# One fused attention kernel: some of VectorE's integer adds on GpSimd, planner constants, and a re-ordered end

## The chip, the core and the metric

The kernel runs on one core of one Trainium2 chip. The metric is the device time of one execution in microseconds; lower is better. A core has five engines that run their own instruction streams and meet at semaphores: TensorE (PE in the profile; its weight loads are PEld), VectorE (DVE), ScalarE (ACT), GpSimd (POOL) and SyncE (SP), which here issues most of the transfers.

## What is computed

Two attention blocks read the same x (2,048 rows of 512). Block A is softmax attention with 32 heads of width 16, block B is linear attention with the same heads, and a gate per row mixes them. Cut to what matters:

```python
qkv = (x @ wqkv).reshape(B, S, 3, H, Dh).transpose(2, 0, 3, 1, 4)
# A
scores = einsum("bhqd,bhkd->bhqk", q, k) * Dh ** -0.5
a = (einsum("bhqk,bhkd->bhqd", softmax(scores), v)) @ wo_A
# B
phi = lambda t: where(t > 0, t + 1, exp(t)) + 1e-6
kv = einsum("bhsd,bhse->bhde", phi(k), v); z = phi(k) summed over s
b = (einsum("bhqd,bhde->bhqe", phi(q), kv) / (phi(q) . z + 1e-6)) @ wo_B
g = sigmoid((x * gate_w).sum(-1))
out = g * a + (1 - g) * b
```

## The kernel before

**Units and rounds.** The scores of block A are cut into 2,048 units. A unit is one product of 128 keys by 512 queries of one head, and fills one PSUM bank (128 x 512, float32). 64 units make a round (one query chunk, four heads), and there are 32 rounds. The main loop goes over groups of units: two slots of three banks (`SLOTS`) take turns; TensorE fills the banks of a slot, ScalarE raises all units of the slot to the exponential in one instruction (L1979, 1,024 or 1,536 columns) and writes them to the tile PT, and TensorE multiplies them with the values (`pv_cols`, into one accumulator bank) while ScalarE works on the other slot.

**Claimed units.** VectorE takes a part of the units from ScalarE. `claim` gives a unit to VectorE; the operation at L1518 scales a PSUM bank and writes it as 16-bit integers into a buffer of the tile DP, and these bits are read as 16-bit floats, a piecewise-linear approximation of the exponential. Four claimed units share one buffer (a group, `tri`, 2,048 columns). To make the approximation better, `try_close` writes two more copies of the whole buffer with a constant added to the integers (`STEPS` 342 and 683, the operation at L1566), in two further buffers, and TensorE sums the three with scaled values. So a claimed unit needs three value products where a unit of ScalarE needs one. There are 13 buffers (`NB`); `free_buffers` lists those that nothing reads or writes any more. `claim_round` takes a unit of the current round while at least 14 (`MIN_LEFT`) of its units are left, and of the next round after that.

**The planner.** The order of all instructions is fixed when the kernel is built. The builder keeps an estimated clock for each engine (`E.t`), with an estimated duration for each operation. VectorE's work waits in a list (`items`) with a priority: 0 for the accumulator, 1 for PSUM evictions and claims, 2 for the range check, 3 for the adds; `pump` emits the next one when VectorE's estimated clock falls behind TensorE's. An item can also be marked for GpSimd (a sixth field, its duration); before, these are only the 12 products of normalisation at L1246 (`POOL_TT` = 1.3), which `pool_go` emits behind an add. `est_start` puts a VectorE operation that reads no PSUM bank behind the estimated end of a running GpSimd operation (`pool_runs`); this orders the plan and adds no semaphore. `claim_beside`, `claim_in_group` and `misc_step` decide whether a unit is claimed, by the work that VectorE has queued (`dve_load` against `CLAIM_LOAD`, `RING_LOAD`, `STARVE`). Projections, block B and output products are steps in chains with a due time in groups (`target`, `late`). `misc_step` runs them in TensorE's spare time, and `fill` adds products of a zero tile (`warm`) when TensorE's estimated share of work falls under `MAC_LOW` (`MAC_END` from 44 units of a round on).

The branch for adds on GpSimd exists in `try_close` before the change, but `EVERY = 0` turns it off.

**The end.** After the last round VectorE normalises the last heads into O_sb (L1275), TensorE transposes it, and VectorE adds it into OT (L2050). TensorE finishes the last four output blocks of 128 rows. For two of them (0 and 1) everything but the last product has been summed in `presum`, and VectorE finishes them (L2075). The other two (2 and 3) are finished by ScalarE (L2069). For block 2 seven products are left for the end (`late_fns`). A check (L2055, L2080, L2085) tests whether all row sums were in range; its flag decides a branch on every engine to a general version of the kernel.

Of the kernel before, what the change touches and what calls it, by code (L numbers as in the profile page):

```python
# [53 lines left out]
NTRI = 4  # L54
# [150 lines left out]
def d_sb(n, rate=1.0):  # L205
    return 0.15 + n * 1.042e-3 * rate
# [6 lines left out]
def bass_gated_mix__mha_block__linear_attn_block__prompt_kernel(  # L213
# [29 lines left out]
    PRE_T = 5  # L243
    PRE_GAP = 8
    OUT_GAP = 8

    with ExitStack() as es:
# [62 lines left out]
        dev = SB([128, 2, 128], FP32, "dev")  # L310
        flag = SB([128, 1], I32, "flag")
        epool = SB([128, 2, 512], BF16, "epool")
        KVbd = SB([128, NCC, 128], BF16, "KVbd")
# [81 lines left out]
        r_rraw = [R(f"rraw{k}") for k in range(8)]  # L395
        r_dev, r_flag = R("dev"), R("flag")
        r_e = [R("e0"), R("e1")]
        r_phiK = [[R(f"phiK{s}_{k}") for k in range(4)] for s in range(2)]
# [33 lines left out]
        pool_runs = collections.deque(maxlen=4)  # L432
        POOL_SOON = 0.3
        POOL_TT = 1.3
        POOL_V = 0.9
        POOL_ADD = 2.4
        EVERY = 0
        OT_POOL = 1
# [37 lines left out]

        def pool_go(sync):

            for it in sorted(items, key=lambda i: i.seq):
                o = it.ops[0]  # L480
                if len(o) > 5 and not blocked(it, o[1], o[2]) and est_start(PO, o[1], o[2]) <= DV.t + POOL_SOON:
                    STATS["pool"] = STATS.get("pool", 0) + 1
                    emit_item_op(it, sync)
                    return
# [48 lines left out]

        WAIT_BANK = 0.12

        def pump(now, look=0.25):
            try_close()
            while items and DV.t <= now + look:
                best = None
                for it in items:  # L540
                    o = it.ops[0]
                    if len(o) > 5 or blocked(it, o[1], o[2]):
                        continue
                    st = est_start(DV, o[1], o[2])
                    wait = st - DV.t
                    key = (wait > (WAIT_BANK if it.prio <= 1 else 0.12), it.prio, st, it.seq)
                    if best is None or key < best[0]:
                        best = (key, it, st)
                if best is None:
                    return  # L550
                if best[2] > now + look + WAIT_BANK:
                    return
                emit_item_op(best[1])

        def dve_load(now):
# [137 lines left out]

        op(PO, lambda: nc.gpsimd.memset(warm[:], 0.0), writes=[r_warm])  # L694
        op(PO, lambda: nc.gpsimd.memset(identb[:], 0.0), writes=[r_ident])
        op(PO, lambda: nc.gpsimd.affine_select(out=identb[:], in_=identb[:], compare_op=ALU.not_equal,
# [195 lines left out]
        GATE_N = 1  # L892
        GATE_AT = 4.5
        GATE_MAC = 0.45
# [389 lines left out]

        PT_URGENT = 11

# [168 lines left out]
        tri = [None]  # L1455
        closing = [None]
        z1_out = [None, None]
        ntri = [0]
# [15 lines left out]
        def can_claim(now, js):  # L1474

            r = claim_round()
            if r is None:
                return None
            t8, qc, half = rounds[r]
            if (t8, qc, half) not in q_done or (t8, 3) not in k_ready:  # L1480
                return None
            u = next((u for u in range(NU - 1, 4 * KB2 - 1, -1) if u >= head[r] and u % 4 in js and u not in taken[r]), None)
            if u is None:
                return None
            kt, q, rd = unit_aps(r, u)
            for res in rd:
                if res.pend or res.w is None or res.tw + LAT > now:
                    return None
            if not try_close() and (tri[0] is None or len(tri[0][1]) == NTRI - 1):
                return None  # L1490
            if tri[0] is None and len(free_buffers()) < CLAIM_FREE:
                return None
            return r, u
# [3 lines left out]
        def free_buffers():  # L1497

            used = [e[3] for e in pv_pending]
            held_ = [c[0] for c in (tri[0], closing[0]) if c is not None]  # L1500
            free = [i for i in range(NB) if i not in held_ and not any(x.pend or x in used for x in r_DP[i])]
# [26 lines left out]
        def close_tri():  # L1528
            if tri[0] is not None and closing[0] is None:
                closing[0] = (*tri[0], [])  # L1530
                tri[0] = None
            try_close()

        def try_close():

            while closing[0] is not None:
                i, us, zs = closing[0]
                z = len(zs) + 1
                if z == NG4:
                    closing[0] = None  # L1540
                    return True
                free = free_buffers()
                if not free:
                    return False
# [4 lines left out]
                mine_, out_ = r_DP[i][0:len(us)], r_DP[i2][0:len(us)]  # L1549
                if EVERY and z == NG4 - 1 and n == NTU and ntri[0] % EVERY == 0:  # L1550
                    push(3, [(lambda z=z, i2=i2, y=y, n=n: nc.gpsimd.tensor_scalar(
                        DP[:, i2, 0:n].bitcast(I16), y, 1.0, float(STEPS[z]), ALU.mult, ALU.add), mine_, out_, 0.0, None, POOL_ADD)])
                    if z1_out[0] is None:
                        pool_go([])
                    else:
                        z1_out[1] = out_
                else:
                    z1_out[:] = [out_, None]

                    def added(z=z, out_=out_):  # L1560
                        if z1_out[0] is out_:
                            z1_out[0] = None
                        if z == NG4 - 1 or z1_out[1] is not None:
                            z1_out[1] = None
                            pool_go(out_)
                    push(3, [(lambda z=z, i2=i2, y=y, n=n: nc.vector.tensor_single_scalar(DP[:, i2, 0:n].bitcast(I16), y, STEPS[z], ALU.add),  # L1566
                              mine_, out_, d_sb(n, 0.25), added)])
                for k, (r, u) in enumerate(us):
                    add_products(i2, z, k, r, u)
            return True  # L1570


        Q_OFF = 0
        GPR = 15.2
# [197 lines left out]
        ROOM = 0.4  # L1772
        CLAIM_LOAD = 3.3
        LATE_CLAIM = 4.0
        STARVE = 7
        MAC_LOW = 0.47
        MAC_END = 0.45
# [9 lines left out]
        PV_LAG = 14  # L1787
        LATE = 9
        LAG_END = 12
# [229 lines left out]

        while tri[0] is not None or closing[0] is not None:  # L2020
            close_tri()
            if closing[0] is not None and not pv_step(PE.t, force=True):
                flush_items()
# [12 lines left out]
        while pv_pending:  # L2036
            if not pv_step(PE.t, force=True):
# [4 lines left out]
        late_rd = [r_OT[t][lastq] for t in range(NT8 - 1)] + [r_OBT[4 * lastq + 2], r_woA, r_woB]  # L2042
        pe_macro(late_fns[:4], reads=late_rd, writes=[r_bank[free[2]]], dur=4 * MM512)
        tbank = SLOTS[(g + 1) % 2][0]
        trb = bank_ap(tbank).bitcast(BF16)
        pe_macro([f_tr(trb[:, 128 * k:128 * (k + 1)], O_sb[:, k, :]) for k in range(4)], reads=[r_O, r_ident],
                 writes=[r_bank[tbank]], dur=0.3)
        pe_macro(late_fns[4:], reads=late_rd, writes=[r_bank[free[2]]], dur=3 * MM512)
        o_last = OT[:, NT8 - 1, 512 * lastq:512 * (lastq + 1)]
        op(DV, lambda: nc.vector.tensor_tensor(o_last, trb[:, 0:512], o_last, ALU.add),  # L2050
           reads=[r_bank[tbank], r_OT[NT8 - 1][lastq]], writes=[r_OT[NT8 - 1][lastq]], dur=0.68)

# [6 lines left out]
        dp_all += r_outl  # L2059
        order = [k for pair in zip(range(NPRE, 4), range(NPRE)) for k in pair]  # L2060
        assert len(order) == 4
        for k in order:
            tb = 4 * lastq + k
            pe_macro([f_mm(bank_ap(free[k]), OT[:, NT8 - 1, 128 * tb:128 * (tb + 1)], woA[:, NT8 - 1, :], start=(k < NPRE))],
                     reads=[r_OT[NT8 - 1][lastq], r_woA], writes=[r_bank[free[k]]], dur=MM512)
        for k in range(NPRE, 4):
            o = bank_ap(free[k])
            tb = 4 * lastq + k
            op(AC, lambda k=k, o=o, tb=tb: nc.scalar.activation(outl[:, k, :], o, ACT.Copy, scale=gom[:, 0, tb:tb + 1]),  # L2069
               reads=[r_bank[free[k]], r_g], writes=[r_outl[k]], dur=0.6)  # L2070
            dma(out2[128 * tb:128 * (tb + 1), :], outl[:, k, :], semL[k], reads=[r_outl[k]], total_after=16, E=AC)
        for k in range(NPRE):
# [5 lines left out]
            dma(out2[128 * tb:128 * (tb + 1), :], outl[:, k, :], semL[k], reads=[r_outl[k]], total_after=16, E=SP)  # L2078
            if k == 0:
                op(DV, lambda: nc.vector.scalar_tensor_tensor(out=bad, in0=dev[:, 1, :], scalar=OK_MID - OK_HALF, in1=bad,  # L2080
# [184 lines left out]
```

## Time and profile before

| | |
|---|---|
| median of 3 runs | 702.99 us (702.07 to 703.46) |
| the profiled execution's own time | 702.72 us |
| its span in the profile | 701.0 us |
| busy, ScalarE | 687.5 us (98%) |
| busy, TensorE | 676.9 us (97%) |
| busy, VectorE | 660.2 us (94%) |
| busy, GpSimd | 24.1 us (3%) |

Times in the profile are from one execution. A row of a group names the line, the engine, the operation, the tile written and those read, the count, then the busy time in us and the mean duration in ns, and then the idle time just before with what ended it. Rows of a timeline begin with the start and the duration in us. VectorE's instructions overlap by a little: the next one starts before the one ahead has fully ended, so start-to-start is shorter than the duration.

### The profile page before, as it was taken

The numbers are of one execution on the slowest core, as the hardware profiler recorded it, in microseconds if no ns is written. First come the engines' busy times: TensorE is split into PE (matmuls) and PEld (weight loads), VectorE is DVE, ScalarE is ACT, GpSimd is POOL, SyncE is SP. The second block draws the span as 40 slices with busy tenths as digits, with TensorE's granted clock in tenths as the row PEclk, the third lists the DMA queues.
The fourth block names the chain that finished last, engine by engine and source line by source line (L and its number), as shares of the span: only waits on it lengthen the run. The fifth ranks groups of instructions, "written<-read, shape, count | busy, mean of one in ns | idle before, by whom it ended". The sixth has DMA issues, their size and how long they took to land.

```text
span 701.0 us, 19208 instructions
## 1 busy us (share of the span) xinstructions
PE 676.9 (97%) x8181; PEld 205.6 (29%) x8181; DVE 660.2 (94%) x1140; ACT 687.5 (98%) x710; POOL 24.1 (3%) x31
## 2 busy tenths in 40 slices
PE   8999999999999999999999999999999999999997
PEld 4322223332223323232322232322222222222223
DVE  4599999999999998999999999999999998999995
ACT  6999999999999999999999999999999999999996
POOL 4000000000000000000000000000000000000000
PEclk9999999999999999999999999999999999999999
DMA  9800101000010001201010011101111201010101
GB/s 222 233 2 9 25 2 34 1 14 22 10 24 2 19 16 40 50 7 33 3 22 13 14 37 17 28 15 26 31 25 29 44 13 44 17 41 18 35 23 49
DMA packets 44815, 22.96 MB, mean 33 GB/s; under 512 B 33976, under 2 KB 40568, under 8 KB 44728
## 3 DMA queue, kind: packets, MB, share of 16 engines
q1 hardware_dynamic: 42712, 20.12, 12.7%
q10 hardware_dynamic: 2016, 1.57, 0.9%
q8 instruction: 67, 1.10, 0.7%
q14 instruction: 20, 0.16, 0.1%
HBM read 8.00 MB, written 2.10 MB: 14 GB/s over the span
## 4 chain that ended last, share of the span: by engine, by line
ACT 93%; PE 6%; DVE 1%; issue 0%; POOL 0%; ACTq 0%; POOLq 0%
ACT PT L1979 90%; PE ps L646 6%; ACT epool L929 2%; DVE DP L2075 0%; DVE xT L1847 0%; PE ps L653 0%; DVE KT L818 0%; DVE DP L2080 0%; DVE flag L2085 0%; POOL warm L694 0%; POOL dummy L663 0%; ACT eg L913 0%; ACTq L2188 0%; POOLq L2250 0%
## 5 line engine op out<-in xcount | busy, mean ns | idle before, releaser
L1979 ACT ACTIVATE PT<-ps 128x1024 bf16<-128x1024 f32 (+1 forms) x670 | 679.7, 1337 | 0.6 <-PE ps L646 0.5
L1518 DVE TENSOR_SCALAR DP<-ps 128x512 int16<-128x512 f32 x584 | 384.5, 683 | 13.4 <-PE ps L646 10.5
L646 PE MATMUL ps<-Qpad,KT 32*128 32x512 bf16 x2048 | 269.1, 384 | 17.6 <-ACT PT L1979 12.8
L1566 DVE TENSOR_SCALAR DP<-DP 128x2048 int16<-128x2048 int16 x292 | 193.8, 682 | 0.0
L646 PE MATMUL ps<-DP,Vaug 128*32 128x512 f16 x1741 | 188.1, 384 | 0.3 <-DVE oraw L1258 0.3
L646 PE MATMUL ps<-PT,Vaug 128*32 128x512 bf16 x1451 | 163.5, 385 | 0.6 <-DVE Vaug L873 0.5
L646 PEld LDWEIGHTS ps<-Qpad,KT 32*128 32x128 bf16 x2048 | 67.3, 91 | 289.1 <-ACT PT L1979 265.7
L646 PE MATMUL ps<-warm 128*32 128x512 bf16 (+1 forms) x510 | 72.8, 384 | 1.1 <-POOL warm L694 1.1
L646 PEld LDWEIGHTS ps<-DP,Vaug 128*32 128x32 bf16 x1741 | 46.4, 95 | 58.5 <-issue 34.0
L646 PEld LDWEIGHTS ps<-PT,Vaug 128*32 128x32 bf16 x1451 | 38.9, 94 | 52.4 <-issue 40.6
L1246 POOL TENSOR_TENSOR OT<-oraw,rbc 128x512 bf16<-128x512 f32 x12 | 15.6, 1303 | 524.5 <-DVE DP L1566 524.5
L646 PE MATMUL ps<-xT,wA 128*32 128x512 bf16 x432 | 32.1, 384 | 0.0
L929 ACT ACTIVATE epool<-ps 128x512 bf16<-128x512 f32 x32 | 27.4, 858 | 0.0
L646 PEld LDWEIGHTS ps<-warm 128*32 128x32 bf16 (+1 forms) x510 | 18.8, 97 | 19.8 <-issue 15.2
L1258 DVE COPY oraw<-ps 128x512 f32<-128x512 f32 x31 | 21.1, 682 | 0.1
L646 PE MATMUL ps<-wB,xT 128*32 128x512 bf16 x256 | 19.3, 384 | 0.0
L646 PE MATMUL ps<-xT,wB 128*32 128x512 bf16 x256 | 18.8, 383 | 0.0
L646 PE MATMUL ps<-woA,OT 128*32 128x512 bf16 (+1 forms) x226 | 18.6, 383 | 0.0
L934 DVE SCALAR_TENSOR_TENSOR phi<-ps,epool 128x512 bf16<-128x512 f32 x24 | 16.3, 680 | 0.0
L818 DVE CAST KT<-ps 128x512 bf16<-128x512 f32 (+1 forms) x16 | 10.7, 667 | 4.9 <-PE ps L646 4.9
L646 PE MATMUL ps<-wA,xT 128*128 128x128 bf16 x192 | 14.9, 220 | 0.0
L873 DVE CAST Vaug<-ps 128x512 bf16<-128x512 f32 x16 | 10.9, 683 | 2.3 <-PE ps L646 2.3
(104 smaller groups left out, 233.1 us busy)
## 6 DMA issues: line engine op xcount, KB each, us to landing
rbc<-oraw SPq DMA_DIRECT2D x16, 256.0 KB
OT<-in_A_x_dram SPq DMA_DIRECT2D x4, 512.0 KB, 7.2
Qpad<-Qs SPq DMA_DIRECT2D x124, 16.0 KB, 1.8
oraw<-oraw SPq DMA_DIRECT2D x60, 32.0 KB, 2.0
wA<-in_A_wqkv_dram SPq DMA_DIRECT2D x1, 1536.0 KB, 7.8
wB<-in_B_wqkv_dram SPq DMA_DIRECT2D x1, 1536.0 KB, 9.0
out_dram<-outt SPq DMA_DIRECT2D x12, 128.0 KB, 1.8
phi<-in_A_x_dram ACTq DMA_DIRECT2D x3, 256.0 KB, 6.1
```

What stands on the lines that cost most here:

```text
L646: return lambda: nc.tensor.matmul(o, lhsT=l, rhs=r, start=start, stop=stop, skip_group_check=sg)
L818: push(1, [(lambda: nc.vector.tensor_copy(KT[:, par, c0:c1], src), [r_bank[b]], [r_KT[par][t]], d_psum(n), None)])
L873: ops = [(lambda: nc.vector.tensor_copy(v_group(NQC * par + v)[:, :, :, 0:16], src), [r_bank[b]], [r_V[par][v]], d_psum(512), lambda: v_do ...
L929: op(AC, lambda: nc.scalar.activation(epool[:, s, :], bank_ap(b), ACT.Exp), reads=[r_bank[b]], writes=[r_e[s]], dur=0.6, issue=0.48)
L934: (lambda: nc.vector.scalar_tensor_tensor(out=dst, in0=bank_ap(b), scalar=0.0, in1=epool[:, s, :], op0=ALU.max, op1=ALU.add), [r_bank[b], ...
L1246: push(1, [(lambda: (nc.gpsimd if on_pool else nc.vector).tensor_tensor(OT[:, t8, 512 * qc:512 * (qc + 1)], oraw[:, 0, :], rbc[:], ALU.mul ...
L1258: push(0, [(lambda: nc.vector.tensor_copy(oraw[:, half, :], acc), [r_acc], [r_oraw[half]], d_psum(512), evicted)])
L1518: push(0 if in_group else 1, [(lambda: nc.vector.tensor_scalar(DP[:, i, 512 * k:512 * (k + 1)].bitcast(I16), bank_ap(b), FRAC - Y_BIAS4, Y ...
L1566: push(3, [(lambda z=z, i2=i2, y=y, n=n: nc.vector.tensor_single_scalar(DP[:, i2, 0:n].bitcast(I16), y, STEPS[z], ALU.add), mine_, out_, d ...
L1979: op(AC, lambda p0=p0, b0=b0, n=n: nc.scalar.activation(PT[:, 512 * p0:512 * p0 + n], ps[:, 512 * b0:512 * b0 + n], ACT.Exp, scale=LN2 / F ...
```

## The change

`EVERY` becomes 2: of every second group of four, the second add (683) goes to GpSimd, if all its units are of the round that ScalarE is in, that is not the last round, and more than 22 units of it (`POOL_LEFT`) are not claimed. The GpSimd operation handles pairs of 16-bit integers as 1,024 32-bit integers and adds a pair constant from a small tile (`step2`), in place of 2,048 16-bit ones with a scalar. The planner's duration for it (`POOL_ADD`) goes from 2.4 to 1.97. `pool_go` is called around every emission of VectorE. If an add for VectorE is ready, that one is emitted first (`boost`), and the GpSimd operation then waits for it (`last_add`).

Closed groups stand in a queue in place of a single place (`closing`), and the adds of a group of a later round than the one being accumulated wait until no other add is queued (`early`). With `MOST_OPEN = 0` a group isn't filled beyond three units while one is still open, as before. `RUSH = 0` leaves its rule off.

Constants change: `PRE_GAP` 8 to 6, `GATE_AT` 4.5 to 3.5, `PT_URGENT` 11 to 12, `Q_OFF` 0 to -4, `CLAIM_LOAD` 3.3 to 3.7, `STARVE` 7 to 6, `MAC_LOW` 0.47 to 0.45, `LATE` 9 to 8.

At the end, the seven `late_fns` are no longer put four ahead of the transposes and three behind. `late_until` puts as many as fit by the planner's clock ahead of the transposes, then ahead of the last products, and the rest ahead of block 2. The last products go in the order 3, 0, 1, 2, ScalarE finishes 3 and then 2, the store of block 3 is issued by SyncE, and the last part of the range check is emitted behind VectorE's second output and not its first.

```diff
-        POOL_ADD = 2.4
-        EVERY = 0
+        POOL_ADD = 1.97
+        EVERY = 2
+        POOL_LEFT = 22
...
-        def pool_go(sync):
+        def pool_go(sync=None):
...
+                    if not last_add[1] and any(x.prio == 3 and len(x.ops[0]) == 5 and not blocked(x, x.ops[0][1], x.ops[0][2])
+                                               for x in items):
+                        boost[0] = True
+                        return
+                    boost[0] = last_add[1] = False
                     STATS["pool"] = STATS.get("pool", 0) + 1
-                    emit_item_op(it, sync)
+                    emit_item_op(it, last_add[0])
...
         def pump(now, look=0.25):
             try_close()
+            pool_go()
...
-                    key = (wait > (WAIT_BANK if it.prio <= 1 else 0.12), it.prio, st, it.seq)
+                    key = (wait > (WAIT_BANK if it.prio <= 1 else 0.12), -1 if it.prio == 3 and (boost[0] or (RUSH and it.ops[0][5:] == () and due_now(it))) else it.prio, st, it.seq)
...
                 emit_item_op(best[1])
+                pool_go()
...
+                early = us[0][0] > acc_round[0]
+                if len(free) < (LAZY if early else 1):
+                    return False
+                if not zs and sum(1 for it in items if it.prio == 3) >= (1 if early else MOST_ADDS):
                     return False
...
-                if EVERY and z == NG4 - 1 and n == NTU and ntri[0] % EVERY == 0:
-                    push(3, [(lambda z=z, i2=i2, y=y, n=n: nc.gpsimd.tensor_scalar(
-                        DP[:, i2, 0:n].bitcast(I16), y, 1.0, float(STEPS[z]), ALU.mult, ALU.add), mine_, out_, 0.0, None, POOL_ADD)])
+                if (EVERY and z == NG4 - 1 and n == NTU and ntri[0] % EVERY == 0 and us[0][0] == us[-1][0] < NR - 1
+                        and us[0][0] == act_round[0] and NU - len(taken[us[0][0]]) > POOL_LEFT):
+                    push(3, [(lambda z=z, i2=i2, y=DP[:, i, 0:n].bitcast(I32), n=n: nc.gpsimd.tensor_tensor(
+                        DP[:, i2, 0:n].bitcast(I32), y, step2[:].bitcast(I32).to_broadcast([128, n // 2]), ALU.add),
+                        mine_ + [r_step], out_, 0.0, None, POOL_ADD)])
                 else:
...
+                    def added(out_=out_):
+                        last_add[:] = [out_, True]
+                        boost[0] = False
...
-        pe_macro(late_fns[:4], reads=late_rd, writes=[r_bank[free[2]]], dur=4 * MM512)
+        late_fns = collections.deque(late_fns)
+
+        def late_until(t):
+            n = min(len(late_fns), max(0, int((t - PE.t) / MM512 + 0.4)))
+            if n:
+                pe_macro([late_fns.popleft() for _ in range(n)], reads=late_rd, writes=[r_bank[free[2]]], dur=n * MM512)
+        late_until(r_O.tw + LAT - 0.25)
...
-        pe_macro(late_fns[4:], reads=late_rd, writes=[r_bank[free[2]]], dur=3 * MM512)
...
-           reads=[r_bank[tbank], r_OT[NT8 - 1][lastq]], writes=[r_OT[NT8 - 1][lastq]], dur=0.68)
+           reads=[r_bank[tbank], r_OT[NT8 - 1][lastq]], writes=[r_OT[NT8 - 1][lastq]], dur=0.45)
+
+        late_until(r_OT[NT8 - 1][lastq].tw + LAT)
...
-        for k in order:
+        assert NPRE == 2
+        for k in (3, 0, 1, 2):
             tb = 4 * lastq + k
+            if k == 2:
+                late_until(PE.t + 10.0)
...
-        for k in range(NPRE, 4):
+        for k in (3, 2):
...
-            dma(out2[128 * tb:128 * (tb + 1), :], outl[:, k, :], semL[k], reads=[r_outl[k]], total_after=16, E=AC)
+            dma(out2[128 * tb:128 * (tb + 1), :], outl[:, k, :], semL[k], reads=[r_outl[k]], total_after=16, E=SP if k == 3 else AC)
...
-            if k == 0:
+            if k == NPRE - 1:
```

## Prediction

> **What bounds the kernel now.** I read the page first: busy shares and the chain that ended last.
>
> ```profile
> span 701.0 us, 19208 instructions
> ...
> PE 676.9 (97%) x8181; PEld 205.6 (29%) x8181; DVE 660.2 (94%) x1140; ACT 687.5 (98%) x710; POOL 24.1 (3%) x31
> ...
> ACT 93%; PE 6%; DVE 1%; issue 0%; POOL 0%; ACTq 0%; POOLq 0%
> ```
>
> ScalarE is busy 98% of the span and the chain lies on it for 93%: the time is the number of units that ScalarE exponentiates. GpSimd has 24.1 us of work in 701. Next, the costliest groups (line, engine, operation, tiles, count, then busy us and mean ns):
>
> ```profile
> L1979 ACT ACTIVATE PT<-ps 128x1024 bf16<-128x1024 f32 (+1 forms) x670 | 679.7, 1337 | 0.6 <-PE ps L646 0.5
> L1518 DVE TENSOR_SCALAR DP<-ps 128x512 int16<-128x512 f32 x584 | 384.5, 683 | 13.4 <-PE ps L646 10.5
> L646 PE MATMUL ps<-Qpad,KT 32*128 32x512 bf16 x2048 | 269.1, 384 | 17.6 <-ACT PT L1979 12.8
> L1566 DVE TENSOR_SCALAR DP<-DP 128x2048 int16<-128x2048 int16 x292 | 193.8, 682 | 0.0
> ...
> L646 PE MATMUL ps<-warm 128*32 128x512 bf16 (+1 forms) x510 | 72.8, 384 | 1.1 <-POOL warm L694 1.1
> ```
>
> There are 2,048 score units. VectorE claims 584 of them (L1518) and ScalarE does the other 1,464 in 679.7 us, 0.46 us each. ScalarE is idle 0.6 us before them, so only one thing makes the middle shorter: more units claimed by VectorE. What lets it claim more is VectorE time. The windows view for 40 to 640 us (columns: window, length, then busy us with counts for PE, PEld, DVE, ACT, POOL, and clock, DMA share, GB/s) shows how full it is:
>
> ```profile
> 40.00:640.00 600.00, 583.01 (x7024) 171.74 (x7022) 584.27 (x1004) 600.00 (x626) 15.64 (x12) 1.00 0.10 22
> ```
>
> ScalarE has no gap at all, VectorE 15.7 us of idle time in 600, and TensorE 17.0, with filler products (the warm row) counted as work.
>
> **Adds on GpSimd.** A group of four claims is followed by two adds, so the 292 adds make 146 groups. The change sends the second add of every second group to GpSimd if the group lies wholly in the round that ScalarE is in. From the page, 584/32 = 18.25 claims fall on a round and 45.75 units on ScalarE. A claim goes to the next round once fewer than 14 units are left: that phase is 14/45.75 = 0.31 of a round, and the remaining 0.69 holds 12.7 claims, or 3.16 groups. Over 31 rounds that is 98 groups, and half of them 49 adds. The bounds are 40 (some groups close late) and 73 (half of all groups).
>
> What one costs and frees follows from the 12 products that already run on GpSimd (count, then minimum, median and maximum in ns), with VectorE's timeline around the last of them:
>
> ```profile
> L1246 POOL TENSOR_TENSOR OT<-oraw,rbc x12: 1268/1277/1597, 85.4 to 548.4; 128x512 bf16<-128x512 f32 x12
> ```
>
> ```profile
> 548.45 1.28 POOL L1246 TENSOR_TENSOR OT<-oraw,rbc 128x512 bf16<-128x512 f32 x1 [37.41 <-DVE DP L1566]
> ```
>
> ```profile
> 547.62 0.68 DVE L1566 TENSOR_SCALAR DP<-DP 128x2048 int16<-128x2048 int16 x1
> 548.22 0.68 DVE L1518 TENSOR_SCALAR DP<-ps 128x512 int16<-128x512 f32 x1
> 548.82 0.68 DVE L1057 TENSOR_TENSOR OB<-ps,rdB 128x512 bf16<-128x512 f32 x1
> 549.68 1.32 DVE L1518 TENSOR_SCALAR DP<-ps 128x512 int16<-128x512 f32 x2 [0.18 <-PE ps L646]
> ```
>
> An add and a PSUM eviction both begin 0.60 us after the operation ahead, so an add that goes frees 0.60 us and a claim costs 6/4 of that, 0.90 us with its adds. Evictions beside the GpSimd operation stay at 0.68 us: they are not slowed. But in that stretch VectorE may run only operations that read PSUM, and it runs out of them: 0.18 us here, 0.23 in the first such stretch, 1.03 in the worst.
>
> ```profile
> 86.68 0.69 DVE L1518 TENSOR_SCALAR DP<-ps 128x512 int16<-128x512 f32 x1 [0.23 <-PE ps L646]
> ```
>
> ```profile
> 463.51 0.69 DVE L1518 TENSOR_SCALAR DP<-ps 128x512 int16<-128x512 f32 x1 [1.03 <-PE ps L646]
> ```
>
> Eight of the twelve stretches have such a gap, 3.64 us in all, 0.30 us for each of the twelve. Prolonged from 1.28 us to 1.97 us, the planner's figure for the new add, the twelve stretches hold the same gaps, because PSUM evictions follow in them almost throughout. The added rule that lets a ready VectorE add pass first, with evictions waiting behind it, fills the stretch better, so I take 0.20 us of idle. Net is 0.40 us for each add, between 0 (all of it lost) and 0.60 (none lost): 49 x 0.40 = 19.6 us of VectorE time.
>
> That time isn't all gain, since a shorter span gives VectorE less time. With n more claims the span falls by 0.46 n, and VectorE needs 0.90 n = 19.6 - 0.46 n, so n = 14 and the span falls by 6.6 us. In general the span falls by 0.34 us for each us freed: between 0 and 10 us for 0 to 0.60 per add.
>
> The length of the GpSimd add is not in the trace. It has 1,024 pairs of 32-bit integers, the product 512 elements: so 1.28 us if it costs the same as that and 2.55 if twice as much. I take the planner's 1.97, since its figure for the product is 1.30 where the row has 1.277. The Trainium skill, GPSIMD Engine Reference, section 3.1, gives 4,497 ns for a two-input add of 2,048 elements; half of that, 2.25 us, is an estimate from that page. By it the stretch would be 0.28 us longer than planned, 13.7 us in 49, and most of the gain would be gone (the lock rival below).
>
> TensorE carries the claims: one more claimed unit takes three value products instead of one. Four such products run side by side in about 0.22 us, so 14 units cost 14 x 2 x 0.055 = 1.5 us, beside 6.6 us less span. The cover is the fillers, 72.8 us by the warm row, and 17 us of idle time. The filler threshold falls from 0.47 to 0.45, a value that the plan of before already uses late in each round, and the granted clock is 1.00 over the whole window, so I count no loss.
>
> **Other constants.** A larger claim load (3.3 to 3.7), a later bound for lateness, an earlier gate and earlier query steps shift the order. They can touch only VectorE's idle time outside the twelve stretches, 15.7 - 3.6 = 12 us. Taking a third of it gives 4 x 0.34 = 1.4 us; the bounds are 4 us of span either way. The query steps' DMAs on the SP queue go out about four groups earlier, and that queue's loads in the window have a DMA share of 0.10: no cost. Buffers are held longer by 49 slower adds; the waiting work is TensorE's and has the fillers as its cover. If that cover goes, claims are refused for want of two free buffers, which takes gain away.
>
> **The end.** VectorE, TensorE, ScalarE, SP, and the time of a store from issue to landing:
>
> ```profile
> 694.02 0.42 DVE L1275 TENSOR_TENSOR Osb<-ps,rraw 128x256 bf16<-128x256 f32 x1
> ```
>
> ```profile
> 694.18 1.02 PE L646 MATMUL ps<-woB,OBT 128*128 128x512 bf16 x4
> 695.04 0.39 PE L653 MATMUL ps<-identb,Osb 128*128 128x128 bf16 x4
> 695.26 1.72 PE L646 MATMUL ps<-woA,OT 128*128 128x512 bf16 x7
> ```
>
> ```profile
> 696.37 0.69 ACT L2069 ACTIVATE DP<-ps,gom 128x512 bf16<-128x512 f32 x1 [3.51 <-PE ps L646]
> 697.09 0.38 ACTq L569 DMA_DIRECT2D out_dram<-DP  x1
> 697.52 0.69 ACT L2069 ACTIVATE DP<-ps,gom 128x512 bf16<-128x512 f32 x1 [0.46 <-ACT DP L2069]
> 698.23 0.38 ACTq L569 DMA_DIRECT2D out_dram<-DP  x1
> ```
>
> ```profile
> 697.37 1.20 SPq L569 DMA_DIRECT2D out_dram<-DP  x2
> ```
>
> ```profile
> 698.12 0.27 DVE L2085 TENSOR_REDUCE flag<-ps 1x1 int32<-1x128 f32 x1
> ```
>
> ```profile
> out_dram<-DP ACTq DMA_DIRECT2D x2, 128.0 KB, 2.0
> ```
>
> The last head's result stands at 694.44, but its transposes start at 695.04, behind four output products: up to 0.5 us goes. ScalarE's first output (now block 3) no longer waits behind all late products, and its second no longer behind 0.46 us for the issue of the first store. That store moves to SP, where two others take 0.60 us each; it is ready before them, and VectorE's second output arrives after the first two are issued. So the last ScalarE store goes out 0.4 to 0.6 us earlier than 698.23. It lands 2.0 later, at 700.2 now, near the end. The range check is the other end: put behind VectorE's second output it waits for 0.75 us more, with nothing behind it on VectorE but the branch of every engine; the earlier start gives about as much back, so its last operation stays near 698.4. I take 0.4 us of gain, between 0 and 0.7.
>
> **The sum.** The profiled execution took 702.72 us (span 701.0 and 1.7 around it); the median of the runs is 702.99. Sum: -6.6 - 1.4 - 0.4 = -8.4: 694.3 for the profiled execution and 694.6 for the median.
>
> **The rivals.**
>
> *More than that (683 to 690).* Adds pass first so regularly that GpSimd's stretches always find evictions, and 60 to 73 adds are moved: 0.60 x 65 x 0.34 = 13 us, with the rest 15 to 20 us less. For it: four of the twelve stretches show no gap without any such rule. Against it: evictions can wait only in the few PSUM banks outside ScalarE's two sets.
>
> *Slower: the port lock.* A GpSimd operation and a VectorE operation that reads and writes SBUF alone do not run together:
>
> ```profile
> 415.15 1.60 POOL L1246 TENSOR_TENSOR OT<-oraw,rbc 128x512 bf16<-128x512 f32 x1 [36.08 <-DVE DP L1566]
> ```
>
> ```profile
> 414.32 1.29 DVE L1566 TENSOR_SCALAR DP<-DP 128x2048 int16<-128x2048 int16 x2
> ```
>
> This product began beside the second add, which ended at 415.61, and took 0.32 us longer than its sisters. The Trainium skill, SBUF — State Buffer, "SBUF: two separate sides", calls this an exclusive lock held for the whole instruction, the loser blocked; by that rule the trace agrees (1.597 against 1.277 us). If the new add takes 2.55 us where 1.97 is planned, the next VectorE add, which the planner sets just behind the stretch, stands 0.58 us, and behind it the evictions that free ScalarE's banks. 49 x 0.58 = 28 us fall into an order laid out for 14 more claims. VectorE's idle time takes up to 15 of them, the rest stands in front of ScalarE: 694.6 + 13 = 708, up to 718 if less is absorbed. It decides from an overrun near 0.45 us, an add of 2.4 us. For it: the row's per-element cost doubled. Against it: an integer add is another operation than a float product, and the planner's other figures are close to the trace.
>
> *No change.* Few groups qualify, or the freed time is lost to gaps: 0.60 us of idle per stretch gives 0, and the constants cancel: 702 to 704.
>
> **How the numbers follow.** A measurement of this kernel tells about 0.2% (1.4 us) from no change. My forecast (691 to 701 us, likeliest 694.6) gets 0.58, more than that 0.16, no change 0.05, slower 0.21. All of the first two is faster by over 0.2%: 0.74. The range 684 to 708 takes in the bounds above and the nearer half of the slower case; about 0.15 lies outside.
>
> **What would show it.** About 49 GpSimd adds of close to 1.97 us, each beginning shortly after a VectorE add; about 250 VectorE adds (292 and seven for 14 more claims, less 49); 598 claims; ScalarE at 1,450 units and still without gaps; evictions beside GpSimd at 0.68 us. At the end, transposes at once behind the last result. ScalarE waiting for TensorE or VectorE inside the window, or VectorE adds well over 0.68 us, would make it wrong, and so would GpSimd adds of 2.4 us and more.

## Result, and the profile after

| | before | changed |
|---|---|---|
| median of 6 runs | 702.92 us (702.02 to 703.46) | 697.83 us (697.38 to 698.36) |
| ratio to before | | 0.993, interval 0.9917 to 0.9943 |
| the profiled execution's own time | 702.72 us | 698.09 us |
| its span | 701.0 us | 696.3 us |

The change makes the kernel 5.1 us faster, between 4.0 and 5.8 by the interval. The forecast was 8.4 us.

The page of the changed kernel: its busy shares, the chain that ended last, and the groups that answer to those of before (line numbers have moved: ScalarE's exponential is now L1999, VectorE's claim L1536, its add L1585, and the new GpSimd add L1578):

```profile
span 696.3 us, 19208 instructions
...
PE 673.1 (97%) x8162; PEld 203.8 (29%) x8164; DVE 642.0 (92%) x1099; ACT 682.5 (98%) x707; POOL 139.9 (20%) x91
...
ACT 85%; PE 14%; DVE 0%; issue 0%; POOL 0%; ACTq 0%; POOLq 0%
...
L1999 ACT ACTIVATE PT<-ps 128x1024 bf16<-128x1024 f32 (+1 forms) x667 | 673.8, 1321 | 1.4 <-PE ps L664 1.3
L1536 DVE TENSOR_SCALAR DP<-ps 128x512 int16<-128x512 f32 x596 | 392.0, 684 | 23.7 <-PE ps L664 19.7
...
L1578 POOL TENSOR_TENSOR DP<-DP,step 128x1024 int32<-128x1024 int32 x59 | 115.2, 1953 | 437.7 <-DVE DP L1536 335.6
...
L1585 DVE TENSOR_SCALAR DP<-DP 128x2048 int16<-128x2048 int16 x239 | 159.6, 689 | 0.0
```

59 adds have gone to GpSimd, VectorE's adds fall from 292 to 239, and claims rise from 584 to 596, so ScalarE has 12 units fewer. The chain that ended last lies on TensorE for 14% of the span where it was 6%. VectorE is less busy (642.0 for 660.2 us), and waits 19.7 us for TensorE before claims where it waited 10.5. The window from 40 to 640 us says the same (busy us in the order PE, PEld, DVE, ACT, POOL):

```profile
40.00:640.00 600.00, 584.56 (x7054) 170.91 (x7051) 574.74 (x978) 599.25 (x629) 127.63 (x69) 1.00 0.10 22
```

VectorE's idle time there is 25.3 us where it was 15.7. The windows view over exactly the stretches in which GpSimd runs its product (before, 12 stretches) and its add (after, 59) shows where it lies; these are the rows with the sums:

```profile
sum 15.64, PE 15.62 PEld 4.29 DVE 12.65 ACT 15.64 POOL 15.60; mean PE 1.30 PEld 0.36 DVE 1.05 ACT 1.30 POOL 1.30
```

```profile
sum 115.11, PE 112.03 PEld 31.73 DVE 103.74 ACT 114.81 POOL 115.00; mean PE 1.90 PEld 0.54 DVE 1.76 ACT 1.95 POOL 1.95
```

VectorE idles 3.0 us in the 12 stretches of before (0.25 us for each) and 11.4 us in the 59 of after (0.19 us for each).

The end, on ScalarE and TensorE:

```profile
686.80 2.21 ACT L1999 ACTIVATE PT<-ps 128x1536 bf16<-128x1536 f32 x2
691.89 1.33 ACT L2097 ACTIVATE DP<-ps,gom 128x512 bf16<-128x512 f32 x2 [2.88 <-PE ps L664]
693.25 0.38 ACTq L587 DMA_DIRECT2D out_dram<-DP  x1
```

```profile
690.55 0.40 PE L671 MATMUL ps<-identb,Osb 128*128 128x128 bf16 x4
```

The last exponential ends at 689.01, so 7.3 us lie behind it. Before, it was 8.1 (692.86 to 701.0). The span's 4.7 us thus come as 3.85 ahead of the end and about 0.8 from the end.

### The profile page after: what moved, and what is told of

The parts are those of the page before. It is cut to its first block, busy times and chain, and to the rows that moved or that the text cites. A ratio compares the mean times of both kernels' runs of the same rounds, so it can differ in the third digit from the quotient of the medians.

```text
span 696.3 us, 19208 instructions
## 1 busy us (share of the span) xinstructions
PE 673.1 (97%) x8162; PEld 203.8 (29%) x8164; DVE 642.0 (92%) x1099; ACT 682.5 (98%) x707; POOL 139.9 (20%) x91
## 4 chain that ended last, share of the span: by engine, by line
ACT 85%; PE 14%; DVE 0%; issue 0%; POOL 0%; ACTq 0%; POOLq 0%
ACT PT L1999 83%; PE ps L664 13%; ACT epool L948 2%; PE ps L671 0%; DVE DP L2103 0%; DVE KT L837 0%; DVE flag L2113 0%; DVE DP L2108 0%; POOL warm L712 0%; POOL dummy L681 0%; ACT eg L932 0%; POOL step L713 0%; ACTq L2216 0%; POOLq L2278 0%
## 5 line engine op out<-in xcount | busy, mean ns | idle before, releaser
L1999 ACT ACTIVATE PT<-ps 128x1024 bf16<-128x1024 f32 (+1 forms) x667 | 673.8, 1321 | 1.4 <-PE ps L664 1.3
L1536 DVE TENSOR_SCALAR DP<-ps 128x512 int16<-128x512 f32 x596 | 392.0, 684 | 23.7 <-PE ps L664 19.7
L664 PE MATMUL ps<-DP,Vaug 128*32 128x512 f16 x1779 | 203.3, 385 | 0.4 <-DVE DP L1536 0.2
L1578 POOL TENSOR_TENSOR DP<-DP,step 128x1024 int32<-128x1024 int32 x59 | 115.2, 1953 | 437.7 <-DVE DP L1536 335.6
L664 PE MATMUL ps<-PT,Vaug 128*32 128x512 bf16 x1435 | 176.7, 385 | 0.9 <-DVE oraw L1277 0.5
L1585 DVE TENSOR_SCALAR DP<-DP 128x2048 int16<-128x2048 int16 x239 | 159.6, 689 | 0.0
L664 PEld LDWEIGHTS ps<-DP,Vaug 128*32 128x32 bf16 x1779 | 48.7, 94 | 62.9 <-issue 37.8
L664 PE MATMUL ps<-warm 128*32 128x512 bf16 (+1 forms) x463 | 62.0, 385 | 1.1 <-POOL step L713 1.1
L664 PEld LDWEIGHTS ps<-PT,Vaug 128*32 128x32 bf16 x1435 | 42.4, 94 | 56.2 <-issue 45.0
L664 PEld LDWEIGHTS ps<-warm 128*32 128x32 bf16 (+1 forms) x463 | 16.2, 97 | 13.2 <-issue 9.8
```

Of the source, the lines that this page charges most:

```text
L664: return lambda: nc.tensor.matmul(o, lhsT=l, rhs=r, start=start, stop=stop, skip_group_check=sg)
L1536: push(0 if in_group else 1, [(lambda: nc.vector.tensor_scalar(DP[:, i, 512 * k:512 * (k + 1)].bitcast(I16), bank_ap(b), FRAC - Y_BIAS4, Y ...
L1578: push(3, [(lambda z=z, i2=i2, y=DP[:, i, 0:n].bitcast(I32), n=n: nc.gpsimd.tensor_tensor(DP[:, i2, 0:n].bitcast(I32), y, step2[:].bitcast ...
L1999: op(AC, lambda p0=p0, b0=b0, n=n: nc.scalar.activation(PT[:, 512 * p0:512 * p0 + n], ps[:, 512 * b0:512 * b0 + n], ACT.Exp, scale=LN2 / F ...
```

## Experiments

**The end alone.**

> The kernel before with the edits of the end alone (late products in the pauses, block 3 stored by SyncE, the check last). The prediction's step: 0.4 us faster, between 0 and 0.7. The rival: the end is worth more than that, since the stretch behind ScalarE's last exponential fell from 8.1 to 7.3 us in the changed kernel, so 0.8 us. Nothing before the end should move: 584 claims, the same VectorE idle time.

```diff
 before.py, with the end of the changed kernel:
+        late_until(r_O.tw + LAT - 0.25)
...
+        for k in (3, 0, 1, 2):
...
+            ... E=SP if k == 3 else AC)
```

701.62 us, ratio 0.9986 (0.9977 to 0.9995): 1.0 us faster, between 0.35 and 1.6. ScalarE's timeline of this kernel:

```profile
687.63 4.78 ACT L1979 ACTIVATE PT<-ps 128x1536 bf16<-128x1536 f32 x4
...
697.41 0.38 ACTq L569 DMA_DIRECT2D out_dram<-DP  x1
```

The exponential ends at 692.41 and the span (699.7) 7.3 us later, as in the changed kernel. ScalarE's last store is issued 5.00 us behind the exponential, where it was 5.37 (698.23 - 692.86). The rival of this expectation holds: 0.8 us, not 0.4.

**The GpSimd adds alone, with the old constants and the old end.**

> The changed kernel with the eight constants and the end set back: the GpSimd adds and the queue of groups alone. Theory A, by the prediction: VectorE's time is what limits the claims, so 59 adds free 59 x 0.4 = 24 us and the kernel gains most of what the full change gains: 697 to 699 us. Theory B: adds on GpSimd free VectorE time that the old constants do not turn into claims, so the count of claims stays at 584 and the time is 702 or more, up to 706 if ScalarE waits for banks.

```diff
 the changed kernel, with the end of before and
-        CLAIM_LOAD = 3.7, STARVE = 6.0, MAC_LOW = 0.45, LATE = 8, Q_OFF = -4, PT_URGENT = 12, GATE_AT = 3.5, PRE_GAP = 6
+        CLAIM_LOAD = 3.3, STARVE = 7,   MAC_LOW = 0.47, LATE = 9, Q_OFF = 0,  PT_URGENT = 11, GATE_AT = 4.5, PRE_GAP = 8
```

705.03 us, ratio 1.0033 (1.0021 to 1.0045): slower than before, although the same 59 adds have left VectorE. Its page, its window, and the sum over its 59 stretches:

```profile
L1536 DVE TENSOR_SCALAR DP<-ps 128x512 int16<-128x512 f32 x584 | 382.8, 684 | 32.0 <-PE ps L664 28.3
```

```profile
40.00:640.00 600.00, 579.61 (x6917) 170.08 (x6914) 559.04 (x948) 597.99 (x625) 124.46 (x67) 1.00 0.10 22
```

```profile
sum 115.71, PE 112.19 PEld 32.36 DVE 97.09 ACT 115.71 POOL 115.61; mean PE 1.90 PEld 0.55 DVE 1.65 ACT 1.96 POOL 1.96
```

Not one claim more than before. The freed time has become idle time: 41.0 us in the window where it was 15.7, and 18.6 us of VectorE's idle time lie in the stretches (0.32 us each). ScalarE even has 2.0 us of gaps in the window where it had none. Theory B holds here; theory A, the prediction's, falls.

**The rest of the change without the adds, and the eight constants alone.**

> The changed kernel with EVERY = 0: new constants, new queue of groups, new end, all adds on VectorE. Theory A: without the adds the gain is gone but for the end, 701.5 to 703. Theory B: part of the gain comes from constants and queue, 700 or less.

> The kernel before with the eight new constants alone. The prediction's step put the constants at 1.4 us of gain within 4 either way, so 701.5. Theory B: the constants do nothing without the adds, 702 to 704.

```diff
 the changed kernel:                 before.py:
-        EVERY = 2                   -        the eight old constants
+        EVERY = 0                   +        the eight new constants
```

Without the adds: 703.40 us, ratio 1.001 (1.0001 to 1.0019), 581 claims. The constants alone: 703.09 us, ratio 1.0002 (0.9993 to 1.0011), 583 claims. So neither gains anything alone, and with the new constants the adds are worth 703.4 - 697.8 = 5.6 us and 15 claims. The first of the two kernels also has the new end, worth 1.0 us alone, and the new queue of groups. By subtraction (703.40 + 1.0 - 703.09) the queue without adds costs some 1.3 us; no run has it alone.

**Another setting of the constants, with and without the adds.**

> The changed kernel with seven of the eight constants set back and only the gate's due time (3.5) as in the change. Its plan has 594 claims. Theory C: the adds are worth some 3 to 5 us at most settings of the constants, and the old set is a poor spot for the plan with adds: 698 to 700. Theory D: the change needs just its own set of constants, and elsewhere the adds bring nothing: 702 or more.

> The same kernel as the one with the gate's due time alone, but EVERY = 0. Its plan has 573 claims. Theory C: slower than its partner by 3 us or more, 704 to 708, although no constant differs. Theory D: the same as its partner within 1.5 us.

```diff
 the changed kernel with seven of the eight constants set back (GATE_AT = 3.5 stays), and
   EVERY = 2      |      EVERY = 0
```

With the adds 699.98 us (ratio 0.9958, 0.9944 to 0.9972), without them 706.23 us (1.0048, 1.0034 to 1.0062). The groups of claims, with and without:

```profile
L1536 DVE TENSOR_SCALAR DP<-ps 128x512 int16<-128x512 f32 x594 | 389.1, 684 | 25.6 <-PE ps L664 21.7
```

```profile
L1536 DVE TENSOR_SCALAR DP<-ps 128x512 int16<-128x512 f32 x573 | 376.3, 684 | 19.9 <-PE ps L664 16.6
```

21 claims and 6.25 us. Three pairs that differ in the adds alone or nearly so now stand side by side:

| constants | claims without, with adds | time without, with adds | per claim |
|---|---|---|---|
| old | 584, 584 | 702.8, 705.0 | |
| old, but the gate earlier | 573, 594 | 706.2, 700.0 | 0.30 us |
| new | 581, 596 | 703.4, 697.8 | 0.37 us |

The first pair has the old end, and its queue of groups differs too; the others have the new end. Theory C holds: the adds are worth 5 to 6 us at two settings of three, and the old set is a poor spot for them. The plans without adds differ as well (573 to 584 claims), so each of these numbers is the difference of two plans, and part of the 6.2 us belongs to a poor partner (706.2 us, 3.4 more than at the old constants). In the last two pairs the time follows the count of claims; in the first the count stays and ScalarE's 2.0 us of gaps are added. What a freed microsecond brings in claims changes from spot to spot.

**How long GpSimd's add takes.** Three kernels have the changed kernel's order of instructions and another add.

> The changed kernel with the same order of instructions, but the GpSimd add as a scalar add over 2,048 16-bit integers, for which the planner of before had 2.4 us; the plan still reckons with 1.97. Lock theory: VectorE adds that the plan puts just behind the stretch are blocked by the overrun, 59 x 0.4 to 0.5 = 24 to 30 us, of which idle time takes half: 705 to 715 us, with VectorE adds well over 0.68 us. Rival: VectorE has slack at these places and the time stays within 1 us of 697.8.

```diff
-  nc.gpsimd.tensor_tensor(DP[...].bitcast(I32), y, step2[:]...to_broadcast([128, n // 2]), ALU.add)
+  nc.gpsimd.tensor_scalar(DP[...].bitcast(I16), y.bitcast(I16), 1.0, float(STEPS[2]), ALU.mult, ALU.add)
```

697.04 us, ratio 0.9923 (0.991 to 0.9936). The premise failed: the operation isn't longer. Its row (minimum, median, maximum in ns), and below it that of the changed kernel:

```profile
L1578 POOL TENSOR_SCALAR DP<-DP x59: 1894/1897/2400, 43.9 to 653.9; 128x2048 int16<-128x2048 int16 x59
```

```profile
L1578 POOL TENSOR_TENSOR DP<-DP,step x59: 1890/1892/2397, 44.0 to 653.9; 128x1024 int32<-128x1024 int32 x59
```

So this run is only a repetition of the changed kernel with another operation, and tells nothing on the lock.

> The changed kernel with the same order of instructions, but from the 24th group on the GpSimd add handles only the first half of the columns; the other half of the third copy is left as it was, so part of the computation is left out. GpSimd's add falls from 1.89 to about 1.0 us. If the length of the stretch on the chip costs time (blocked VectorE adds, late buffers), the time falls by 1 us or more, below 697. If only the order laid out by the planner counts, with VectorE kept on evictions, it stays at 697.4 to 698.2, and the gaps of VectorE stay.

```diff
-  DP[:, i2, 0:n]  from  y = DP[:, i, 0:n]
+  DP[:, i2, 0:m]  from  y = DP[:, i, 0:m],  m = n if ntri[0] < 24 else n // 2
```

697.58 us, ratio 0.9927 (0.9915 to 0.994), with a median GpSimd add of 1.04 us. In this order of instructions an add of half the length brings nothing, so the chip loses no measurable time to the length of the add itself; in the changed kernel TensorE's weight loads wait for these adds only 7 times, 2.0 us in all. The run can't tell why VectorE gets no more claims, since the order fixes the 596 claims. No run has a plan that reckons with a shorter add, or with more than 13 buffers.

> The changed kernel with the same order of instructions and the same sums, but each GpSimd add cut into four operations of 256 integers one behind the other. By the two lengths seen (1.89 us for 1,024 and 1.04 for 512 integers) a piece takes about 0.61, so the add takes about 2.45 us or a little more, where the plan reckons with 1.97. The prediction's slower rival priced this at 28 us of blocked VectorE time and 705 to 718 us. Against it: VectorE has gaps at these places in the changed kernel, 11 us within the stretches, which would take up part: 699 to 703. If the time stays under 699, an overrun of 0.5 us costs nothing and the rival's turning point of 2.4 us was wrong.

```diff
+  for c in range(0, n // 2, n // 8):
+      h = nc.gpsimd.tensor_tensor(out[:, c:c + m], y[:, c:c + m], step2..., ALU.add)     # m = n // 8
```

698.20 us, ratio 0.9936 (0.9922 to 0.995). The first add of this kernel on GpSimd's timeline, four pieces as one block:

```profile
44.01 2.32 POOL L1580 TENSOR_TENSOR DP<-DP,step 128x256 int32<-128x256 int32 x4 [34.38 <-DVE DP L1536]
```

The add takes 2.32 us, not 2.45: 0.43 more than in the changed kernel and 0.35 more than planned. In 59 adds that is 21 to 25 us more on GpSimd, and the time is 0.4 to 1.2 us above the three runs of the same order (697.04, 697.58, 697.83), less than the intervals can tell. So overruns of this size are absorbed.

**The planner without the avoidance.**

> The changed kernel with a planner that doesn't keep VectorE's SBUF operations out of GpSimd's stretches. Its plan has 600 claims and not 596. Lock theory: VectorE adds meet running GpSimd operations and block for up to 1.9 us, or GpSimd waits for them; the claims come late and ScalarE waits: 699 to 706 us, although ScalarE has fewer units. No lock: 695 to 696 us, VectorE adds all near 0.68 us and GpSimd adds all near 1.89 us.

```diff
-            if E is DV and not any(res in r_bank for res in reads):
+            if False:
```

717.78 us in the median, ratio 1.0203 (1.016 to 1.0246). The six runs lie far apart: 711.24 to 722.70 us, with a granted clock of 0.995 in the fastest and 0.973 in the slowest, where no run of the other kernels is under 0.996. The profiled one took 712.12 us at 0.995. VectorE's adds, and ScalarE's waits:

```profile
L1585 DVE TENSOR_SCALAR DP<-DP x246: 622/682/2404, 35.0 to 695.2; 128x2048 int16<-128x2048 int16 x123
```

```profile
ACT PT L1999 <- PE ps L664: 13.0, 26, 1.1
```

An add that takes 0.68 us alone now takes up to 2.40 us (1.64 at most in the changed kernel), and ScalarE waits 13.0 us for TensorE where it waited 1.3, with four units fewer. The lock theory holds, at a higher price than expected: 14 us between the profiled executions (712.12 and 698.09), 20 between the medians. How much of it comes with the lower clock is open, and the plan isn't the same (54 GpSimd adds, not 59).

**More adds.**

> The changed kernel with EVERY = 1: every group whose units are of the current round gives its second add to GpSimd, about 110 adds for 59. By the prediction's rule (0.34 us for each us freed, 0.40 us an add) another 50 adds would bring 6.9 us: 691. Rival: with twice as many stretches VectorE finds no evictions for them, its freed time turns into gaps, and TensorE's steps come late because banks are held: 702 to 708, with VectorE idle well above the 25 us of the changed kernel in the window from 40 to 640 us.

```diff
-        EVERY = 2
+        EVERY = 1
```

704.23 us, ratio 1.0021 (1.0012 to 1.003). 110 adds on GpSimd, and the window:

```profile
40.00:640.00 600.00, 587.31 (x6888) 172.64 (x6885) 539.85 (x909) 596.90 (x639) 218.37 (x117) 1.00 0.10 21
```

```profile
sum 212.69, PE 208.82 PEld 60.72 DVE 188.41 ACT 210.34 POOL 212.50; mean PE 1.90 PEld 0.55 DVE 1.71 ACT 1.91 POOL 1.93
```

VectorE is idle 60.2 us in the window, and only 24.3 of its idle time in the whole span lies in the 110 stretches (second row). There are 592 claims, fewer than the 596 of the changed kernel, and ScalarE has gaps of 3.1 us. The forecast of the rival holds, but most of the idle time lies outside the stretches. The largest piece is here:

```profile
340.00:400.00 60.00, 59.92 (x741) 17.60 (x735) 35.74 (x57) 59.62 (x63) 12.58 (x7) 1.00 0.14 30
```

In these 60 us VectorE is idle for 24.3 us, while TensorE is busy for 59.92 and runs no filler product at all.

**Other constants with the adds.**

> The changed kernel with eleven constants of the planner set otherwise, among them CLAIM_LOAD and MAC_LOW back at 3.3 and 0.47; the constants were chosen for the planner's own estimated end, 2.7 us earlier than that of the changed kernel, with 597 claims and 60 GpSimd adds. If the order laid out decides, as the runs with other constants showed, it gives 694 to 696.5 us and beats both kernels. If the new claim load was what the adds needed, it is slower than the changed kernel, 698 or more.

```diff
-  PRE_T = 5, PRE_GAP = 6, OUT_GAP = 8, POOL_SOON = 0.3, POOL_LEFT = 22, MIN_LEFT_LAST = 20, B1 = 21, HURRY = 40,
-  CLAIM_LOAD = 3.7, MAC_LOW = 0.45, END_FROM = 44, RING_LOAD = 4, LEND = 120, LAG_END = 12
+  PRE_T = 7, PRE_GAP = 8, OUT_GAP = 6, POOL_SOON = 0.5, POOL_LEFT = 24, MIN_LEFT_LAST = 16, B1 = 22, HURRY = 46,
+  CLAIM_LOAD = 3.3, MAC_LOW = 0.47, END_FROM = 40, RING_LOAD = 4.4, LEND = 200, LAG_END = 10
```

(Fourteen constants in all, not the eleven of the expectation.) 698.17 us, ratio 0.9939 (0.9926 to 0.9953), with 597 claims and 60 adds. The time lies in the second branch of the expectation, but 0.3 us above the changed kernel is less than the intervals can tell, so neither branch is met cleanly. The planner's 2.7 us did not come over to the chip; but the gain is there with the old `CLAIM_LOAD` and `MAC_LOW`, so it isn't these two constants that the adds need. No plan that clearly beats the changed kernel was found.

## Why the prediction was right, and where it was off

The direction, and a time inside the range, were right; the gain was forecast 1.6 times too large.

*What bounds the kernel: right, but for one stretch.* 12 claims more took 5.0 us of ScalarE's work (687.5 to 682.5 busy), 0.41 us for each where 0.46 was reckoned. ScalarE was to stay without gaps; it has 0.75 us of them in the window, and in the stretch shown below the chain passes to TensorE.

*Count and length of the adds: close.* 59 adds for 49 (bounds 40 to 73), of 1.89 us in the median and 1.95 in the mean for 1.97. Half of the 4,497 ns that the Trainium skill, GPSIMD Engine Reference, section 3.1, gives for a two-input add of 2,048 32-bit floats was an estimate of 2.25 us; the trace decides for 1.89, and a one-input 16-bit add of twice as many elements takes the same 1.90.

*The gap in a stretch: right here.* 0.20 us was assumed and 0.19 measured, so 0.41 us is freed net for the 0.40 assumed. But the gap depends on the order and not on the add alone: it is 0.32 with the old constants.

*From freed time to claims: the step that failed.* The prediction had VectorE's time alone decide the claims, 0.34 us of span for each us freed. With 59 x 0.41 = 24 us freed that rule gives 8.2 us, and 18 claims. Measured were 12 claims and 3.85 us ahead of the end in the full change, no claim and no gain (2.2 us slower) with the old constants, and no gain from 110 adds. Where freed time is left in these kernels is shown: it is idle time, 9.5 us more of it in the window of the changed kernel, 25 us more with the old constants, 44 us more with 110 adds. What refuses the claims is only partly shown. One stretch of the changed kernel stands out, from 280 to 340 us (first before, then after):

```profile
280.00:340.00 60.00, 59.44 (x749) 17.06 (x745) 57.76 (x98) 60.00 (x62) 2.55 (x2) 1.00 0.12 27
```

```profile
280.00:340.00 60.00, 59.90 (x766) 17.92 (x763) 51.42 (x87) 59.79 (x61) 12.39 (x7) 1.00 0.12 27
```

There block B's large products (those that sum phi(k) times x over all rows) fall due, TensorE is busy 59.90 of 60 us, and VectorE idles 8.6 us for 2.2. That is 6.3 of the 9.5 us. The chain that ended last lies on TensorE there (start, duration), where before it lay on ScalarE from 215.32 to 341.19:

```profile
274.70 10.00 PE ps L664 x130
...
284.72 17.80 PE ps L664 x220
...
302.55 20.93 PE ps L664 x258
...
323.50 14.21 PE ps L664 x191
```

The prediction counted the fillers as TensorE's cover for the claims. That holds for the whole span and not for this stretch: it has no filler product, before or after. In the kernel with 110 adds block B's large products run later, and the idle stretch goes with them, to 340 to 400 us. No run moved these products alone, so that TensorE is the limit there is read from the traces and not tested. With the old constants TensorE has 1.9 us idle from 280 to 340 us and VectorE 8.4, so it isn't the only cause. The prediction also named claims refused for want of free buffers; no run tested that.

*Other constants: wrong.* They were put at 1.4 us of gain; alone they gave 0.3 us the other way, which can't be told from no change. With the adds they count for much more: 584 claims with the old set, 594 with the gate's due time alone changed, 596 with all eight. A sum of separate terms has no place for that.

*The end: right in direction, too small.* 0.4 us (0 to 0.7) forecast, 0.8 in the traces and 1.0 in the runs. The transposes start 0.07 us behind the result (690.55, the result of the last head at 690.48), as said. In the kernel with the end alone ScalarE's last store goes out 0.4 us earlier behind the exponential, as forecast, and still the end is 0.8 us shorter. In the changed kernel it goes out 1.1 us earlier (4.24 us for 5.37), and the end is no shorter than that. So the mis-sized term isn't the issue of this store but the wait behind it. These are waits of SyncE at the very end, before and after (what it waited for, then the us in total, the count and the longest):

```profile
SPq L2224 <- DMA out_dram<-DP: 1.1, 1, 1.1
```

```profile
SPq L2235 <- DVE flag L2113: 0.4, 1, 0.4
```

Before, SyncE stands 1.1 us until the last store has landed. After, it waits for no store there (0.2 us in the kernel with the end alone); ahead of the point where all engines meet it waits for the flag of the range check. So the wait for the last store goes altogether, and the check, which the prediction called the other end, sets the end now; its flag is ready 5.29 us behind the exponential (694.30) where it was 5.53 (698.39). The 0.60 us that the prediction took for the issue of a store on SyncE is half of a row that holds a wait: one issue of these takes 0.34 us.

*The slower rival: the mechanism is real, the price was wrong.* The run without avoidance shows the lock. By the Trainium skill, SBUF — State Buffer, "SBUF: two separate sides", of two operations that need the port pair shared by VectorE and GpSimd the second is blocked for the whole instruction of the first; the trace agrees, with a VectorE add at 2.40 us, about the 1.89 of GpSimd's and its own 0.68 less a little overlap. But the assumption that the planner sets the next add just behind the stretch, so that an overrun is paid in every stretch, is not borne out: 0.35 us over plan cost at most about 1 us. The turning point of 2.4 us itself wasn't passed.

## What to carry to other kernels

Work taken from a full engine is gain only where the schedule can hand that engine something else at that moment. Before counting freed time as throughput, look in each stretch for what would have to supply it, here the order laid out beforehand and, it seems, a TensorE that is full for 60 us. In a kernel whose order a planner lays out, one pair of runs prices an edit badly: 59 adds made the kernel 5.6 and 6.2 us faster and 2.2 us slower at three settings of other constants, so try an edit at several settings before believing or dropping it.

## What was unexpected of the hardware

GpSimd adds a constant to 2,048 16-bit integers per partition in 1.897 us (one tensor input) and to 1,024 32-bit ones in 1.892 us (two inputs, one of them a broadcast pair): packing pairs into 32 bits saved nothing. 512 integers take 1.04 us, and four operations of 256 run back to back in 2.32 us, so a split into four costs 0.43 us.
